# Attention with a bias table in DRAM: shifted rows at one constant distance

## The chip, the cores and the metric

The kernel runs on one core of a Trainium2 chip. The metric is device time of one execution in microseconds; the median of the runs is compared. Inputs and outputs lie in DRAM, and the five engines of the core (TensorE or PE, VectorE or DVE, ScalarE or ACT, GpSimd or POOL, SyncE or SP) run their own instruction streams and meet at semaphores.

## The reference

Attention with a position bias that a small network computes, and behind it a feed-forward part with a cosine gate:

```python
# q, k, v: (4, 8, 576, 64) = batch, heads, positions, head size
scores = scale * np.matmul(q, k.transpose(0, 1, 3, 2))
psi_rel = np.log1p(np.abs(pos[:, None] - pos[None, :]))
psi_i = np.log1p(np.maximum(pos[:, None], 1.0))
x = (psi_rel / psi_i)[..., None]
bias = np.maximum(x @ w1 + b1, 0.0) @ w2        # 32 hidden, 8 heads
scores = scores + bias.transpose(2, 0, 1)[None]
attn = softmax(scores)
x = concat_heads(attn @ v)                      # (2304, 512)
h = x @ w_in                                    # 2048 wide
out = (h * np.cos(h)) @ w_out
```

The bias of a head is a 576 x 576 matrix. It depends on the query position i through `psi_i` and on the distance i - j, and it is the same for all four batches.

## The kernel before, in words

**The bias table.** For one query position the bias of all keys is a window of a row that holds the bias by distance. The kernel computes, for 16 query positions at a time (one of 36 groups), a tile `rt` of 128 rows x 591 numbers: row 8 i + head serves position i of the group and one head. `bias_hid` makes the hidden layer `ht` (three or four instructions on DVE, mostly a fourth on ACT), `bias_rows` multiplies it with the output weights on PE into `pa`, `bias_store` scales it on ACT into `rt` (a pool of 5 buffers) and SP stores it to a DRAM scratch `sc`. Eight groups make one tile t of 128 query positions, `sc[t]`; t = 4 has four groups. The order of the tiles in this stage is 4, 0, 1, 2, 3.

**The load.** `load_bias(hp, t)` fetches the bias of a pair of heads for 128 query positions into `bt` tiles (11 buffers), one for each head: partition i gets the 576 numbers that begin at column 15 - (i mod 16) of its row. The first head is one load of 128 x 576; the second is two loads (64 and 512 columns). For t = 4 both heads share one `bt`, 64 partitions each, one load for each head. The loads for the first pair of heads are issued during the table's stage: t = 4 after row group 11, t = 0 after 19, t = 1 after 27, t = 2 and 3 at its end. The loads for the next pair are issued in the last batch of the pair before it, and used one batch later.

**Attention.** 16 units (4 head pairs x 4 batches), each of 5 slots with the tiles 0, 1, 4, 2, 3. In a slot `qk` multiplies on PE (L390), one DVE instruction for each head adds the bias `bt` and keeps the extreme of each row (L403), ACT does the exponential (L423), POOL divides by the sum (L445), PE turns the result over (L452, L465) and multiplies it with v (L514). The order on every engine is written out in `slot`; PE runs a unit's `qk` ahead of the transposes of the slots before. The first unit has no earlier slots to fill PE with.

**Feed-forward.** The rest, from about 317 us on: two chains of matmuls (L640, L695) on PE, with the gate on ACT and DVE.

**DMA.** All transfers are issued by SP, in program order, with eight semaphores in turn: a transfer waits on SP until the one that was issued eight before it has landed.

Of the kernel before, what the change touches and what calls it, by code (L numbers as in the profile page):

```python
# [9 lines left out]
F32 = mybir.dt.float32  # L10
# [18 lines left out]
def kernel(  # L29
# [11 lines left out]
    nc = tc.nc  # L41
    B, H, S, D = q.shape
# [2 lines left out]
    C = 32  # L45
    HP = H // 2
    NQ = S // 16
    RB = S + 16
    HALF = S // 2
    NF = DFF // 128  # L50
    KD = DM // 128
# [9 lines left out]
    dram = ctx.enter_context(tc.tile_pool(name="dram", bufs=1, space=DRAM))  # L61
# [3 lines left out]
    xT = const.tile([128, HP, NT], F32, name="xT")  # L65
    xs = const.tile([128, 2, KD, TB], F32R, name="xs")
    wpre = [const.tile([128, 2, 2, 512], F32R, name=f"wpre{i}") for i in range(WPRE)]
    sc = [dram.tile([8 if t < 4 else 4, 128, RB], F32, name=f"sc{t}") for t in range(5)]
    groups = [list(range(8 * t, min(8 * t + 8, NQ))) for t in range(5)]

    units = [(hp, b) for hp in range(HP) for b in range(B)]
# [39 lines left out]
    with tc.manual_schedule():  # L111
# [98 lines left out]
        def load_bias(hp, t):  # L210
            if t < 4:
                for h in range(2):
                    bt = bp.tile([128, 576], F32, tag="b", name="bt")
                    src = sc[t]
                    for to, at, n in ((0, 0, S),) if h == 0 else ((0, 512, 64), (64, 0, 512)):
                        nc.sync.dma_start(
                            out=bt[:, to : to + n],
                            in_=bass.AP(
                                src.tensor,
                                src.offset + (2 * hp + h) * RB + 15 + at,  # L220
                                [[128 * RB, 8], [8 * RB - 1, 16], [1, n]],
                            ),
                        )
                    bias[hp, t, h] = bt
            else:
                bt = bp.tile([128, 576], F32, tag="b", name="bt")
                src = sc[t]
                for h in range(2):
                    nc.sync.dma_start(
                        out=bt[64 * h : 64 * h + 64],  # L230
                        in_=bass.AP(
                            src.tensor,
                            src.offset + (2 * hp + h) * RB + 15,
                            [[128 * RB, 4], [8 * RB - 1, 16], [1, S]],
                        ),
                    )
                bias[hp, t, 0] = bt
# [59 lines left out]
        def bias_rows(k, hts):  # L297
            nr = 16 * groups[todo[k][0]][todo[k][1]] + 15
            ps = ps_a.tile([128, 1024], F32, tag="a", name="pa")
            cuts = sorted({0, nr, 512, RB - 1})  # L300
            for a, b in zip(cuts, cuts[1:]):
                for s, ht in enumerate(hts):
                    if a < nr:
                        i = ht[:, nr - b + 1 : nr - a + 1][:, ::-1]
                    else:
                        i = ht[:, a - nr : b - nr]
                    nc.tensor.matmul(  # L307
                        ps[32 * s : 32 * s + 32, a:b],
                        nbd,
                        i,  # L310
                        start=True,
                        stop=True,
                        tile_position=(0, 32 * s),
                    )
            return ps

        def bias_store(k, ps):
            t, gi = todo[k]
            qi = groups[t][gi]
            rt = ra.tile([128, RB], F32, tag="r", name="rt")  # L320
            c = int(k not in ACT_H)
            nc.scalar.activation(  # L322
                out=rt[:, 0 : RB - 1],
                in_=ps[:, 0 : RB - 1],
                func=AF.Identity,
                scale=mrow[:, qi : qi + 1],
                bias=cst[:, c : c + 1],
            )
            nc.sync.dma_start(out=sc[t][gi, :, 0 : RB - 1], in_=rt[:, 0 : RB - 1])

        tiles = [0, 1, 4, 2, 3]
        for i in range(WPRE):
# [6 lines left out]
        for n in range(len(todo) + 1):  # L339
            now = hts  # L340
            if n < len(todo):
                hts = bias_hid(n + 1) if n + 1 < len(todo) else None
                ps = bias_rows(n, now)
            if held:
                bias_store(*held)
            for t in {19: (0,), 27: (1,), 36: (2, 3)}.get(n, ()):
                load_bias(0, t)
            if n == 11:
                load_bias(0, 4)
            held = (n, ps)  # L350
            if n == 6:
                for x in "kq":
                    load(1, x)
            if n in T_FIRST:
                keep_turned(T_FIRST[n][1], turn(*T_FIRST[n], bank()))
            if n in S_FIRST:
                for step in S_FIRST[n][1]:
                    split(0, S_FIRST[n][0], step)
            if n == len(todo):
                abs_w(*wparts[0])  # L360
# [182 lines left out]
        def slot(i):  # L543
# [46 lines left out]
            if now:  # L590
                if i == 1:
                    load(0, "v")
                    load(2, "k")
                for du, x in LOAD_PLAN[j]:
                    if u + du < NU:
                        load(u + du, x)
                hp, b = units[u]
                if b == B - 1 and hp + 1 < HP:
                    load_bias(hp + 1, tiles[j])
                if u == NU - 1 and j < KD:  # L600
                    split_x(0, 0, j)
# [236 lines left out]
```

## Time and profile before

| | |
|---|---|
| runs | 739.06, 742.66 and 959.5 us, median 742.66 |
| the profiled execution | 740.42 us, of which the span from first to last instruction is 738.6 |
| PE | busy 711.1 us, 96% of the span |
| DVE, ACT, POOL | 598.4, 442.5 and 404.3 us |
| mean granted TensorE clock | 0.99 |

The busy shares are means over three stages. In the first 60 us the bias table is made, from 60 to some 317 us attention runs, and from there on the feed-forward part. What a transfer costs is to be read from the stretches in which an engine waited for it, since PE is nearly always busy elsewhere.

### The profile page before, as it was taken

The numbers are of one execution on the slowest core, as the hardware profiler recorded it, in microseconds if no ns is written. First come the engines' busy times: TensorE is split into PE (matmuls) and PEld (weight loads), VectorE is DVE, ScalarE is ACT, GpSimd is POOL, SyncE is SP. The second block draws the span as 40 slices with busy tenths as digits, with TensorE's granted clock in tenths as the row PEclk, the third lists the DMA queues.
The fourth block names the chain that finished last, engine by engine and source line by source line (L and its number), as shares of the span: only waits on it lengthen the run. The fifth ranks groups of instructions, "written<-read, shape, count | busy, mean of one in ns | idle before, by whom it ended". The sixth has DMA issues, their size and how long they took to land.

```text
span 738.6 us, 15708 instructions
## 1 busy us (share of the span) xinstructions
PE 711.1 (96%) x5786; PEld 572.2 (77%) x5786; DVE 598.4 (81%) x1307; ACT 442.5 (60%) x948; POOL 404.3 (55%) x486
## 2 busy tenths in 40 slices
PE   6986999999999999989999999999999999999997
PEld 3764666666666666659899898888888888998985
DVE  8985688889888888846788789898998998966655
ACT  6886678787778888744555555545444454433342
POOL 0204687888877788873546364473555453663300
PEclk9999799999999999999999999999999999999999
DMA  6777426533642640200101010101101010001113
GB/s 200 253 267 194 118 57 159 136 96 92 163 96 67 178 106 18 75 1 1 58 29 58 30 58 28 58 30 48 38 30 57 29 58 29 1 36 51 44 43 87
DMA packets 83918, 58.65 MB, mean 79 GB/s; under 512 B 61824, under 2 KB 70144, under 8 KB 83840
## 3 DMA queue, kind: packets, MB, share of 16 engines
q1 hardware_dynamic: 83840, 57.63, 28.0%
q8 instruction: 46, 0.75, 0.4%
q14 instruction: 32, 0.26, 0.1%
HBM read 42.00 MB, written 15.61 MB: 78 GB/s over the span
## 4 chain that ended last, share of the span: by engine, by line
PE 80%; DMA 8%; DVE 7%; ACT 2%; issue 2%; POOL 0%; SPq 0%; DVEq 0%; ACTq 0%; POOLq 0%
PE ph L640 26%; PE po L695 25%; PE pv L514 10%; PE s L390 9%; DMA bt<-sc 5%; PE pm L452 4%; PE pa L307 3%; DMA sc<-rt 2%; PE pt L465 2%; PE pt L186 1%; DVE P L403 1%; DVE gl L669 1%; DVE ht L291 1%; ACT rt L322 1%; PE spare L186 1%
## 5 line engine op out<-in xcount | busy, mean ns | idle before, releaser
L445 POOL TENSOR_SCALAR P<-P,rc 128x576 f32<-128x576 f32 x144 | 115.3, 813 | 81.1 <-DVE rc L438 33.2
L403 DVE CUSTOM_DVE_ANT_0 P<-s,bt 128x576 f32<-128x576 f32 x144 | 104.1, 754 | 35.9 <-PE s L390 22.1
L644 ACT ACTIVATE a<-ph,quarter 128x384 int32<-128x384 f32 x96 | 55.8, 581 | 108.2 <-PE ph L640 107.0
L650 DVE SCALAR_TENSOR_TENSOR r<-a,ph 128x384 f32<-128x384 int32 x96 | 52.8, 550 | 79.5 <-ACT a L644 79.4
L423 ACT ACTIVATE P<-P,m 128x576 f32<-128x576 f32 x144 | 110.6, 771 | 4.3 <-DVE m L403 3.9
L499 POOL TENSOR_TENSOR xs<-xT,xs 128x384 fp32r<-128x384 f32 x96 | 107.7, 1122 | 8.0
L640 PE MATMUL ph<-xs,wpre 128*128 128x384 f32 x576 | 109.5, 338 | 0.8 <-DVE a L659 0.8
L640 PE MATMUL ph<-xs,w 128*128 128x384 f32 x576 | 108.3, 337 | 0.5 <-DVE a L659 0.5
L640 PEld LDWEIGHTS ph<-xs,wpre 128*128 128x128 f32 x576 | 101.8, 188 | 7.0 <-DVE a L659 2.1
L640 PEld LDWEIGHTS ph<-xs,w 128*128 128x128 f32 x576 | 101.3, 188 | 5.5 <-DVE a L659 1.6
L390 PEld LDWEIGHTS s<-kN,qT 64*128 64x128 f32 (+1 forms) x864 | 71.1, 188 | 43.6 <-DVE m L403 11.0
L655 ACT ACTIVATE r<-r,hpi 128x384 f32<-128x384 f32 x96 | 59.3, 618 | 69.5 <-DVE r L651 69.5
L390 PE MATMUL s<-kN,qT 64*128 64x288 f32 (+1 forms) x864 | 94.3, 316 | 6.4 <-DVE m L403 5.6
L498 POOL TENSOR_SCALAR xs<-xT 128x384 fp32r<-128x384 f32 x96 | 61.8, 644 | 45.3 <-PE ph L640 45.3
L514 PE MATMUL pv<-PT,vN 128*64 128x320 f32 (+1 forms) x512 | 78.5, 429 | 2.3 <-ACT xT L472 2.3
L695 PE MATMUL po<-w,gh 128*128 128x512 f32 x288 | 75.3, 396 | 0.0
L695 PE MATMUL po<-wpre,gh 128*128 128x512 f32 x288 | 75.2, 396 | 0.0
L669 DVE TENSOR_TENSOR gl<-a,gh 128x384 fp32r<-128x384 f32 x96 | 74.4, 775 | 0.6 <-ACT gh L663 0.6
L109 POOL TENSOR_TENSOR w<-wb,w 128x512 fp32r<-128x512 f32 x16 | 20.7, 1296 | 89.9 <-ACT w L107 89.9
L651 DVE SCALAR_TENSOR_TENSOR r<-a,r 128x384 f32<-128x384 int32 x96 | 61.6, 641 | 3.3
L663 ACT ACTIVATE gh<-a 128x384 fp32r<-128x384 f32 x96 | 49.9, 520 | 22.9 <-DVE a L659 22.2
L472 ACT ACTIVATE PT<-pm 128x512 f32<-128x512 f32 (+1 forms) x80 | 44.2, 552 | 30.5 <-PE pm L452 30.1
(83 smaller groups left out, 1205.7 us busy)
## 6 DMA issues: line engine op xcount, KB each, us to landing
sc<-rt SPq DMA_DIRECT2D x36, 295.5 KB
raw<-in_moe_w_in_dram SPq DMA_DIRECT2D x16, 512.0 KB
raw<-in_moe_w_out_dram SPq DMA_DIRECT2D x16, 512.0 KB
bt<-sc SPq DMA_DIRECT2D x16, 288.0 KB
nk<-in_k_dram SPq DMA_DIRECT2D x32, 128.0 KB
nq<-in_q_dram SPq DMA_DIRECT2D x32, 128.0 KB
bt<-sc SPq DMA_DIRECT2D x16, 256.0 KB
vN<-in_v_dram SPq DMA_DIRECT2D x32, 128.0 KB
```

The lines of the kernel that those rows point to most:

```text
L390: nc.tensor.matmul(s[h][:, hf, 0:HALF], qTs[u % 2][r, a, 128 * t : 128 * t + 128] if t < 4 else qTs[u % 2][:, a, 512:640], kN[u][r, b, o : ...
L403: nc.vector.tensor_tensor_reduce(neg.rearrange("p (a x) -> p a x", a=2), s[h][:, :, 0:HALF], bias[hp, t, h].rearrange("p (a x) -> p a x", ...
L423: nc.scalar.activation(out=P[u, j][:, 576 * h : 576 * h + 576], in_=neg, func=AF.Exp, bias=m[:, 0:1], scale=-1.0, accum_out=dn[u, j][:, h ...
L445: nc.gpsimd.tensor_scalar(p, p, r, 1.0, ALU.mult, ALU.mult)
L498: nc.gpsimd.tensor_scalar(h, src, 1.0, 1.0, ALU.mult, ALU.mult)
L499: nc.gpsimd.tensor_tensor(l, src, f(h), ALU.subtract)
L514: nc.tensor.matmul(ps[64 * h : 64 * h + 64, 0 : WQ[hf]], a, m, start=(c == 0), stop=(c == 4), tile_position=(r.start, 64 * h), skip_group_ ...
L640: nc.tensor.matmul(ps, a, x, start=(i == 0), stop=(i == 3 * KD - 1))
L651: nc.vector.scalar_tensor_tensor(r, n, -TWO_PI_LO, r, ALU.mult, ALU.add)
L655: nc.scalar.activation(out=r, in_=r, func=AF.Sin, scale=SIN_SCALE, bias=hpi)
L669: nc.vector.tensor_tensor(gl, a, f(G[key][0]), ALU.subtract)
L695: nc.tensor.matmul(O[n][i], a[:, 128 * i : 128 * i + 128], w, start=(i0 == 0 and p == 0), stop=(i0 == GF - 1 and p == 2),)
```

## The change

The scratch `sc[t]` becomes one row of numbers. A row of the table still has 591 numbers; rows of a group lie 608 numbers apart (`PITCH`), and a group begins 16 x (8 x 608 - 1) numbers behind the one before it (`GP`) where it was 128 x 592. So the start of position i + 1 lies 8 x 608 - 1 numbers behind that of position i for all 128 positions of a tile, over the seams of groups too. The source of a load is then one dimension of 128 rows with n numbers each, where it was 8 groups of 16 rows; for t = 4 it is 64 rows where it was 4 groups of 16. The tile `rt` has 591 columns instead of 592. The numbers that are stored and loaded are the same. Every engine has the same instructions in the same order with the same waits; in the list of SP's transfers the 56 bias loads read 128x576 instead of 128x1x576 (and so on), and nothing else differs.

```diff
-    RB = S + 16
+    RB = S + 15
+    PITCH = S + 32
+    GP = 16 * (8 * PITCH - 1)
...
-    sc = [dram.tile([8 if t < 4 else 4, 128, RB], F32, name=f"sc{t}") for t in range(5)]
+    sc = [dram.tile([1, (8 if t < 4 else 4) * GP + 16], F32, name=f"sc{t}") for t in range(5)]
...
                             in_=bass.AP(
                                 src.tensor,
-                                src.offset + (2 * hp + h) * RB + 15 + at,
-                                [[128 * RB, 8], [8 * RB - 1, 16], [1, n]],
+                                src.offset + (2 * hp + h) * PITCH + 15 + at,
+                                [[8 * PITCH - 1, 128], [1, n]],
                             ),
...
-                            src.offset + (2 * hp + h) * RB + 15,
-                            [[128 * RB, 4], [8 * RB - 1, 16], [1, S]],
+                            src.offset + (2 * hp + h) * PITCH + 15,
+                            [[8 * PITCH - 1, 64], [1, S]],
...
-            cuts = sorted({0, nr, 512, RB - 1})
+            cuts = sorted({0, nr, 512, RB})
...
-                out=rt[:, 0 : RB - 1],
-                in_=ps[:, 0 : RB - 1],
+                out=rt,
+                in_=ps[:, 0:RB],
...
-            nc.sync.dma_start(out=sc[t][gi, :, 0 : RB - 1], in_=rt[:, 0 : RB - 1])
+            nc.sync.dma_start(
+                out=bass.AP(sc[t].tensor, sc[t].offset + gi * GP, [[PITCH, 128], [1, RB]]),
+                in_=rt,
+            )
```

## Rows read from the trace of the kernel before

**Rows 1.** The page, part 4: the chain that ended last, by line.

```profile
PE ph L640 26%; PE po L695 25%; PE pv L514 10%; PE s L390 9%; DMA bt<-sc 5%; PE pm L452 4%; PE pa L307 3%; DMA sc<-rt 2%; PE pt L465 2%; PE pt L186 1%; DVE P L403 1%; DVE gl L669 1%; DVE ht L291 1%; ACT rt L322 1%; PE spare L186 1%
```

**Rows 2.** DMA view, 167.5 to 215.2 us: packets of SP's queue; transfers issued, KB each.

```profile
q1 hardware_dynamic: 12760, 5.84, 51.8%
...
bt<-sc SPq DMA_DIRECT2D x4, 288.0 KB
bt<-sc SPq DMA_DIRECT2D x4, 256.0 KB
vN<-in_v_dram SPq DMA_DIRECT2D x6, 128.0 KB
nq<-in_q_dram SPq DMA_DIRECT2D x6, 128.0 KB
nk<-in_k_dram SPq DMA_DIRECT2D x6, 128.0 KB
raw<-in_moe_w_out_dram SPq DMA_DIRECT2D x1, 512.0 KB
bt<-sc SPq DMA_DIRECT2D x2, 144.0 KB
bt<-sc SPq DMA_DIRECT2D x4, 32.0 KB
vN<-in_v_dram SPq DMA_DIRECT2D x6, 16.0 KB
nk<-in_k_dram SPq DMA_DIRECT2D x3, 32.0 KB
nk<-in_q_dram SPq DMA_DIRECT2D x3, 32.0 KB
```

**Rows 3.** The chain in order of time, 0 to 100 us: start, us, what.

```profile
1.19 3.69 DMA lt<-in_ltab_dram
...
38.98 6.05 DMA sc<-rt
...
60.65 2.90 DMA sc<-rt
...
64.93 8.32 DMA bt<-sc
```

**Rows 4.** Timeline of ACT, 22 to 64 us: start, busy, instruction [idle before, releaser].

```profile
45.14 1.58 ACT L322 ACTIVATE rt<-pa,cst,mrow 128x591 f32<-128x591 f32 x2 [2.54 <-DMA sc<-rt]
...
56.53 2.32 ACT L322 ACTIVATE rt<-pa,cst,mrow 128x591 f32<-128x591 f32 x3 [2.05 <-DMA sc<-rt]
```

**Rows 5.** Timeline of DVE, 22 to 84 us.

```profile
47.27 8.21 DVE L291 TENSOR_SCALAR ht<-lt,edge 128x416 f32<-128x416 f32 x21 [2.28 <-PE pa L307]
60.15 0.76 DVE L403 CUSTOM_DVE_ANT_0 P<-s,bt 128x576 f32<-128x576 f32 x1 [4.67 <-PE s L390]
...
73.42 0.76 DVE L403 CUSTOM_DVE_ANT_0 P<-s,bt 128x576 f32<-128x576 f32 x1 [1.72 <-DMA bt<-sc]
```

**Rows 6.** Windows, four units between their first L403: us, busy (x instructions), clock, DMA.

```profile
75.96:95.08 19.12, 18.08 (x191) 12.51 (x187) 13.42 (x40) 11.94 (x31) 12.42 (x17) 0.84 0.46 110
126.50:142.72 16.22, 15.96 (x184) 10.87 (x182) 13.86 (x40) 13.13 (x35) 12.69 (x17) 1.00 0.64 148
189.96:206.39 16.43, 16.19 (x184) 11.01 (x182) 14.05 (x41) 13.08 (x35) 12.68 (x17) 1.00 0.66 147
253.61:269.31 15.70, 15.70 (x187) 10.84 (x183) 14.08 (x41) 12.62 (x34) 12.91 (x18) 1.00 0.63 156
```

**Rows 7.** Windows around the fall of the clock; columns PE, PEld, DVE, ACT, POOL.

```profile
61.60:71.84 10.24, 7.21 (x80) 5.69 (x81) 7.68 (x22) 8.02 (x23) 7.14 (x10) 1.00 0.74 165
71.84:82.08 10.24, 7.37 (x46) 5.43 (x48) 4.92 (x15) 4.23 (x11) 5.08 (x7) 0.50 0.58 124
```

**Rows 8.** Windows in the table's stage; the last column is GB/s.

```profile
24.00:28.00 4.00, 4.00 (x69) 2.60 (x72) 3.56 (x10) 3.43 (x9) 1.22 (x2) 1.00 0.97 361
41.12:61.60 20.48, 15.74 (x291) 9.67 (x280) 13.36 (x37) 14.95 (x24) 0.00 (x0) 1.00 0.78 272
```

## The prediction

> **What bounds the kernel now.** I read the chain of waits first. It is PE for most of the way, and two DMA lines are the largest things in it that are not PE: the bias loads with 5% and the stores of the table with 2% [rows 1], together some 50 us. That is not what they cost. The chain is followed back through a transfer from its landing to its issue, while PE was mostly at work beside it. So I went on to the views that tell what an engine lost: timelines with the idle time ahead of an instruction, and windows from one attention unit to the next. In the feed-forward part, from about 317 us, no bias load is left; whatever the change does must come from the first 317 us.
>
> Then the question of how a bias load runs. A window of the DMA view that begins and ends in a quiet stretch lets one count [rows 2]. It has 45 transfers. Their rows of data are: bias 12 x 128 and 2 x 64 rows; q, k and v 18 x 512 rows of 256 B; six 16 KB and six 32 KB pieces with 64 and 128 rows; w_out 128 rows. Sum 1536 + 128 + 9216 + 384 + 768 + 128 = 12160. The queue moved 12760 packets, so 600 are not data: one for each DMA engine that ends its share of a transfer. If all 45 ran on 16 engines there would be 720. With 31 others at 16, twelve bias loads at 8 and the two of t = 4 at 4 it is 496 + 96 + 8 = 600, exactly. So a bias load runs on 8 or 4 of 16 engines, the sizes of its outer dimension, and the other transfers, whose outer dimension has 128 or 64 rows, on all.
>
> What that does is seen in the chain: the load of `lt`, also 128 rows of 2304 B, needs 3.69 us, the last bias load before attention 8.32; a store right behind the three loads of t = 0 lands after 6.05 us, one with no load near it after 2.90 [rows 3]. The same engines carry the loads and a half of each store, and what is queued behind waits for them.
>
> **The change, part by part.** The outer dimension becomes 128 (64 for t = 4), so the same data is spread over 16 engines, and a tile's loads occupy an engine half as long, for t = 4 a quarter. Four places gain.
>
> A, the table's stage. ACT fills five `rt` buffers and stands still when the oldest store hasn't landed: 2.54 us before 45.14 and 2.05 before 56.53 [rows 4], behind the loads of t = 0 and t = 1. The first one reaches DVE, the engine that sets the pace there, as 2.28 us of idle time before 47.27. The second falls behind DVE's last `ht` (47.27 + 8.21 = 55.48), where only ACT's stores are left between it and the first `qk`; DVE's first L403 waits for it [rows 5]. The two add: 2.28 + 2.05 = 4.3 us earlier at 60.15. Would a balanced queue still be too slow? DVE makes 21 `ht` in 8.21 us, 3.25 for a row group, so at its undisturbed pace a store of 295.5 KB goes out every 1.27 us, which is 238 GB/s, and a tile's 576 KB of loads in eight groups are 58 more: 296 GB/s. The stage now moves 272, and 361 have been seen over 4 us [rows 8]. So it should fit with little to spare; if 326 were the limit, 5.57 MB of the 20.48 us would need 17.1 and the gain were 3.4. Bounds 2.3 (one wait stays) to 4.6, taken 4.3.
>
> B, the end of the first unit. DVE waits 1.72 us for the load of t = 3 [rows 5]. That load is issued when the last store has landed, and its third piece takes 8.32 us; with 3.69, as for `lt`, it lands 4.6 us earlier [rows 3], more than the wait. The whole stage in front shifts both alike. Taken 1.7, bounds 1 to 2.1.
>
> C, the first unit of each further pair of heads. It takes 16.22, 16.43 and 15.70 us [rows 6]; the third shows the length without a wait. Gain 0.52 + 0.73 = 1.25, bounds 0.8 to 1.3.
>
> D, the clock. [...] With A and B, the same work of the first unit fills 1.7 us less, and the thin time between the last table rows and the second unit shrinks by about 4. I take it that the clock stays up, but this term is all or nothing: 0 or 3.4. [...]
>
> Cost nothing: SP issues the 56 loads at the same places. A shorter issue would only free SP, for which nothing in this argument waits. The loads of q, k and v that are queued behind bias loads lose the less loaded engines and find the others less full; no wait for them stands in this argument. The row distance of 2432 instead of 2368 B leaves the 2364 B that a row writes as they are.
>
> Sum: 4.3 + 1.7 + 1.25 + 3.4 = 10.65 us. Against the profiled execution of 740.42 us that gives 729.8. That execution lies between the two lower runs shown, 739.06 and 742.66, the second of which is the median, so the same 1 or 2 us are uncertain behind the change.
>
> **Rivals.**
> 1. The clock falls all the same: 740.42 - 7.25 = 733.2. For it: the first unit has little for PE to do, and the fall came in its middle. Against it: shorter waits.
> 2. The rate is the limit, not the balance: 16 engines at once pull no more than the 326 to 361 GB/s that were seen, ACT's waits shrink by half, and the clock falls: 740.42 - 2.3 - 1.7 - 1.25 = 735.2.
> 3. The loads don't spread; the split isn't set by the outer dimension. Then nothing changes, 740.4. The count of 600 speaks against it.
> 4. Slower: the stores suffer from the new row distance. The pace of the stage asks 238 GB/s of them; below that the 36 of them set it. At 200 GB/s one takes 1.51 us instead of 1.27, 36 x 0.24 = 8.6 us more, A is gone, and with B and C it is 740.42 + 8.6 - 2.95 = 746.1. For it speaks only that the addresses are new.
>
> [...]
>
> **How the numbers follow.** Forecast (all four terms) 0.50; rival 1 0.27; rival 2 0.13; rival 3 0.06; rival 4 0.04. The predicted time is that of the forecast, 729.8 us. Its own range with the bounds of A to C and the 1 or 2 us between executions is 726 to 733. The range for 8 in 10 goes on through rival 1 and to the edge of rival 2: 726 to 736. Two per cent of 742.66 are 14.9 us, about what a measurement of this kernel can tell from no change; faster by more needs a time below 727.8, which only the lower end of the forecast reaches: 0.16. Slower by over 2% is beyond 757.5, rival 4 at a still lower rate: 0.02. Within: 0.82.
>
> **What would show it.** The packets of SP's queue in the whole program rise by 48 x 8 + 8 x 12 = 480, if all bias loads use 16 engines. ACT's waits for `sc<-rt` (A) and DVE's for `bt<-sc` (B, C) are gone or below a quarter of a microsecond each; the first L403 of DVE stands at about 56 us; the second unit takes some 15.7 us and no window before 317 us has a clock of 0.50 (D). The prediction is wrong if the first L403 comes early and PE's clock falls at another place, or if the stores land later than 3 us with no load near them.

## The result and the profile after

The changed kernel takes 732.16 us (median of 4 runs, 730.09 to 732.7), the kernel before 740.86. The ratio is 0.988, 95% interval 0.985 to 0.992: faster, by some 8.7 us, which is less than 2%. Leaving out executions far off the others (959.5 us here, two of 747 us beside the experiments), before has a median of 739.08 us in the 43 executions beside the experiments (733.82 to 744.69), and the changed program 731.58 in 26 (728.51 to 733.08; 4 of after, 22 of the first four experiments, which came out as the same program): 7.5 us, the better figure for the gain. The profiled execution of after took 731.91 us, 8.51 less than that of before, and its span is 730.1.

**The loads use all 16 DMA engines.** The DMA view of after, over the whole program: packets, MB and share of SP's queue, then transfers with KB each and the median us from issue to landing.

```profile
q1 hardware_dynamic: 84320, 57.63, 27.5%
...
sc<-rt SPq DMA_DIRECT2D x36, 295.5 KB, 3.6
...
bt<-sc SPq DMA_DIRECT2D x16, 288.0 KB, 3.8
...
lt<-in_ltab_dram SPq DMA_DIRECT2D x1, 288.0 KB, 3.9
```

The bytes are the same, the packets 480 more than the 83840 of before, as forecast from the count of [rows 2]. The packets that are not data can be told by their size: in the trace 4960 packets have 4 bytes, 16 for each of SP's 310 transfers; in that of before 4480, which is 254 x 16 + 48 x 8 + 8 x 4, one for each engine as the prediction reads them. A 288 KB bias load lands after 3.8 us, as late as the load of `lt` that has its size.

**Four places, and a fifth.** The timeline of ACT in the table's stage, its two remaining waits for stores (start, busy, instruction, idle before and releaser), which answer to [rows 4]:

```profile
45.53 0.84 ACT L324 ACTIVATE rt<-pa,cst,mrow 128x591 f32<-128x591 f32 x1 [0.48 <-DMA sc<-rt]
...
53.77 3.26 ACT L324 ACTIVATE rt<-pa,cst,mrow 128x591 f32<-128x591 f32 x4 [0.90 <-DMA sc<-rt]
```

And of DVE, answering to [rows 5]:

```profile
48.06 5.82 DVE L293 TENSOR_SCALAR ht<-lt,edge 128x448 f32<-128x448 f32 x15 [0.47 <-PE pa L309]
57.51 0.76 DVE L408 CUSTOM_DVE_ANT_0 P<-s,bt 128x576 f32<-128x576 f32 x1 [3.64 <-PE s L395]
```

The first L408 (L403 before) comes 2.64 us earlier. ACT's waits for stores have shrunk from 6.2 us to 1.4 (view of the tile `sc`), and are not gone. DVE waits for no bias load any more: the view of the tile `bt` names PE and POOL as what DVE waited for, and no DMA.

The windows from unit to unit that answer to [rows 6] (us, busy time of PE, PEld, DVE, ACT, POOL, clock, DMA share, GB/s):

```profile
71.60:89.44 17.84, 17.84 (x189) 12.29 (x185) 13.41 (x40) 11.93 (x31) 12.22 (x16) 0.86 0.40 97
120.86:136.52 15.66, 15.66 (x187) 10.85 (x183) 14.10 (x41) 12.59 (x34) 12.85 (x18) 1.00 0.40 98
183.70:199.68 15.98, 15.95 (x187) 11.02 (x183) 14.33 (x40) 12.60 (x34) 12.88 (x18) 1.00 0.41 96
246.87:262.53 15.66, 15.66 (x187) 10.84 (x183) 14.10 (x41) 12.58 (x34) 12.86 (x18) 1.00 0.40 98
```

The later first units of a pair have lost their waits: 16.22 to 15.66 and 16.43 to 15.98. The second unit, 19.12 before, takes 17.84 with a mean clock of 0.86: the clock fell here too. The windows around it, for [rows 7]:

```profile
59.40:69.64 10.24, 7.60 (x84) 5.77 (x80) 8.38 (x27) 8.66 (x24) 7.57 (x11) 1.00 0.77 200
69.64:76.47 6.83, 6.34 (x42) 4.74 (x44) 3.12 (x9) 2.59 (x7) 4.60 (x6) 0.50 0.52 117
```

It stayed low for 6.83 us where it had been 10.24. The fifth place is the seam from attention to the feed-forward part. The timelines of PE there, of before:

```profile
327.21 3.97 PE L514 MATMUL pv<-PT,vN 128*64 128x320 f32 x16 [2.33 <-ACT xT L472]
```

and of after:

```profile
320.35 2.37 PE L519 MATMUL pv<-PT,vN 128*64 128x320 f32 x16 [2.32 <-ACT xT L477]
```

The same 16 matmuls behind the same wait take 1.6 us less: in the one execution the granted clock was 0.50 from 327.83 to 331.25 us, in the other 1.00 (mean from 313 to 325 us).

The balance of the two spans, 8.54 us: 2.64 up to the first L408, 1.72 in the first unit (15.81 to 14.09), 1.28 in the second, 1.01 in the first units of two pairs, 1.60 at the seam, and 0.29 spread over the rest. Bias loads have gone from 5% of the chain to none among the lines that the page names. Stores of the table are still on it, with 1%; the two large pieces, of the chain in order of time:

```profile
49.43 4.24 DMA sc<-rt
...
54.64 3.19 DMA sc<-rt
```

### The profile page after: what moved, and what is told of

Read it like the earlier page. It is cut to its first block, busy times and chain, and to the rows that moved or that the text cites. A ratio compares the mean times of both kernels' runs of the same rounds, so it can differ in the third digit from the quotient of the medians.

```text
span 730.1 us, 15708 instructions
## 1 busy us (share of the span) xinstructions
PE 708.8 (97%) x5786; PEld 571.9 (78%) x5786; DVE 597.7 (82%) x1307; ACT 441.9 (61%) x948; POOL 403.5 (55%) x486
## 2 busy tenths in 40 slices
DMA packets 84398, 58.65 MB, mean 80 GB/s; under 512 B 62304, under 2 KB 70624, under 8 KB 84320
## 3 DMA queue, kind: packets, MB, share of 16 engines
q1 hardware_dynamic: 84320, 57.63, 27.5%
## 4 chain that ended last, share of the span: by engine, by line
PE 89%; DVE 5%; DMA 2%; issue 1%; ACT 1%; POOL 1%; SPq 0%; DVEq 0%; ACTq 0%
PE ph L645 26%; PE po L700 25%; PE pv L519 12%; PE s L395 11%; PE pm L457 5%; PE pa L309 4%; PE pt L470 2%; PE pt L188 2%; DMA sc<-rt 1%; DVE gl L674 1%; PE spare L188 1%; DVE ht L293 1%; DVE wb L103 1%; DVE acc L723 1%; DMA lt<-in_ltab_dram 1%
## 5 line engine op out<-in xcount | busy, mean ns | idle before, releaser
L450 POOL TENSOR_SCALAR P<-P,rc 128x576 f32<-128x576 f32 x144 | 114.6, 808 | 74.1 <-ACT P L428 29.3
L408 DVE CUSTOM_DVE_ANT_0 P<-s,bt 128x576 f32<-128x576 f32 x144 | 103.8, 754 | 31.1 <-PE s L395 22.5
L519 PE MATMUL pv<-PT,vN 128*64 128x320 f32 (+1 forms) x512 | 76.9, 422 | 2.3 <-ACT xT L477 2.3
```

Of the source, the lines that this page charges most:

```text
L408: nc.vector.tensor_tensor_reduce(neg.rearrange("p (a x) -> p a x", a=2), s[h][:, :, 0:HALF], bias[hp, t, h].rearrange("p (a x) -> p a x", ...
L450: nc.gpsimd.tensor_scalar(p, p, r, 1.0, ALU.mult, ALU.mult)
L519: nc.tensor.matmul(ps[64 * h : 64 * h + 64, 0 : WQ[hf]], a, m, start=(c == 0), stop=(c == 4), tile_position=(r.start, 64 * h), skip_group_ ...
```

## The experiments

The theory: the size of the outer dimension sets how many DMA engines carry a load, and the gain is what the queue of the loaded engines cost. Rival 1: the new row distance does it. Rival 2: a third dimension makes a load slow, whatever its size. The terms of the sum (A, B, C, D) were tested apart. The edits are shown shortened to the places that matter.

**Four kernels that came out as one.** The first four put the groups back into the load, at the constant distance:

```diff
-    [[8 * PITCH - 1, 128], [1, n]],
+    [[16 * (8 * PITCH - 1), 8], [8 * PITCH - 1, 16], [1, n]],    # e1_outer8; 4 of 16 for t = 4
+    [[4 * (8 * PITCH - 1), 32], [8 * PITCH - 1, 4], [1, n]],     # e2_outer32; 16 of 4
+    [[32 * (8 * PITCH - 1), 4], [8 * PITCH - 1, 32], [1, n]],    # e3_outer4; 2 of 32
```

and the fourth, e4_later_pairs, the first of these for the first pair of heads alone.

> The new row distance and the new stores, but the source of a load is again 8 groups of 16 rows (4 of 16 for t = 4), now at the constant distance. Theory (the outer size sets how many DMA engines carry a load): time as before, 740 us (738 to 743), 480 packets fewer than with one dimension, ACT's waits for stores back to about 6 us and DVE's for bias to about 4, first L403 at about 60. Rival 1 (the row distance of 608 numbers did it): time as after, 732. Rival 2 (the number of dimensions makes a load slow): as before, 740, like the theory; the kernel with 32 groups tells these two apart.

> As after, but the source of a load is 32 groups of 4 rows (16 of 4 for t = 4), so it has three dimensions again, with an outer size that 16 divides. Theory: 16 engines, time as after, 732 us (730 to 734), packets 84320. Rival 2 (the third dimension itself costs): 740, waits as before. Rival 1 (row distance): 732 too.

> As after, but 4 groups of 32 rows (2 of 32 for t = 4). Theory: 4 engines (2 for t = 4) carry a load, each twice as long as before. A tile's three loads then hold these engines for about 8 us where they had 4, the stores' rows on the same engines come on top, and a pair of heads needs some 40 us of loads where a unit lasts 15.7: the table's stage 10 to 20 us longer, each of the three changes of pair 15 to 25 us longer, in all 790 to 850 us, and 480 - 208 = 688 packets fewer than after in all (48 x 12 + 8 x 14). Rival 2: 740. Rival 1: 732.

> As after, but the loads for the first pair of heads, which run in the table's stage, have the old 8 groups of 16 (4 of 16). Theory: only the third term of the sum is left, 1 us: time 739.5 (737 to 742), first L403 at about 60 us, DVE waits for bias at the end of the first unit, the later first units of a pair at 15.7 to 16.0 us without a wait. A rival that puts the gain into the later pairs (transfers of q, k and v that land earlier all through attention): 734 or less.

(The 688 packets of the third are 48 x 12 + 8 x 14; the 480 - 208 in its text is a slip.) Measured: 731.65, 732.01, 731.58 and 730.19 us, ratios to before 0.990, 0.991, 0.990 and 0.989, and 84320 packets in each. In these kernels the two dimensions, whose distances fit together, were merged when the kernel was built: SP's transfers read 128x576 in all four, as in after. So the four tell none of the theories apart. They are four more measurements of the changed program, and as such they show how far its executions differ:

| | first L408, us | first two units, us | their mean clock | waits of ACT for stores, us |
|---|---|---|---|---|
| after | 57.51 | 31.93 | 0.89 | 1.4 |
| e1_outer8 | 57.46 | 30.47 | 0.94 | 1.7 |
| e2_outer32 | 58.22 | 30.64 | 0.94 | 3.4 |
| e3_outer4 | 58.65 | 29.33 | 1.00 | 2.4 |
| e4_later_pairs | 57.53 | 29.34 | 1.00 | not named as such |

(In the last, ACT stands idle at the same place, 1.27 us before 53.79, put down to PE.) Before has 60.15, 34.93, 0.85 and 6.2. In the same program the clock fell in the first two units in three of these five executions and stayed up in two.

**Groups that can't be merged.** e5_gap8 leaves 16 numbers unused behind every group:

```diff
-    GP = 16 * (8 * PITCH - 1)
+    GP = 16 * (8 * PITCH - 1) + 16
...
-    [[8 * PITCH - 1, 128], [1, n]],
+    [[GP, 8], [8 * PITCH - 1, 16], [1, n]],      # 4 of 16 for t = 4
```

> The new row distance, the new stores and the tile of 591 columns, but 16 unused numbers behind every group, so that the 8 groups of 16 rows (4 of 16 for t = 4) can't be taken as one dimension; SP's transfers read 128x1x576 again. Theory (the outer size sets how many DMA engines carry a load): time as before, 739 us (736 to 742), 83840 packets, ACT's waits for stores about 6 us, DVE's for bias about 4, first L403 at about 60. Rival 1 (the row distance of 608 numbers did it): 732.

738.02 us, ratio 0.998, interval 0.996 to 1.001: no difference from before. 83840 packets. The view of the tile `sc` (who waited for its transfers, us and times):

```profile
  ACT rt L324: 7.1, 4
  DVE P L408: 1.3, 2
```

Row distance, stores and the tile of 591 columns are those of after, and the gain is gone: rival 1 falls. The slower rival of the prediction falls with the traces: a packet of a stored row (2364 bytes) takes 95 ns in the median in before and in after. DVE's waits are 1.3 us and not the forecast 4; the first L408 came only at 63.27 in this execution, 3 us later than in before, so that the last loads had more time to land; both waits are in later pairs of heads.

e6_gap4 has the unused numbers behind every second group:

```diff
-    sc[t].offset + gi * GP
+    sc[t].offset + gi * GP + gi // 2 * 16
...
-    [[8 * PITCH - 1, 128], [1, n]],
+    [[2 * GP + 16, 4], [8 * PITCH - 1, 32], [1, n]],      # 2 of 32 for t = 4
```

> 16 unused numbers behind every second group: 4 groups of 32 rows (2 of 32 for t = 4). Theory: 4 engines (2 for t = 4) carry a load, 84320 - 688 = 83632 packets. A tile's three loads then hold these engines for some 8 us where they had 4, and a pair of heads needs some 40 us of loads where a unit lasts 15.7: the table's stage and the first unit 15 to 30 us longer, each of the three changes of pair 15 to 25 us longer, in all 790 to 850 us. Rival 2 (a third dimension costs, whatever its size): 739, as with 8 groups.

795.34 us, ratio 1.078, interval 1.075 to 1.081, and 83632 packets, to the packet. The same view for `bt`:

```profile
  DVE P L408: 46.1, 15
```

and the first unit of the second pair of heads, with the one after it:

```profile
137.87:167.00 29.13, 20.27 (x183) 13.92 (x181) 12.77 (x41) 13.82 (x36) 13.32 (x18) 0.79 0.43 118
167.00:184.82 17.82, 17.82 (x191) 12.28 (x187) 13.42 (x41) 11.94 (x31) 12.38 (x17) 0.87 0.32 80
```

A unit that takes 15.66 us with one dimension takes 29.13, with DMA at 0.43 of 16 engines, while DVE waits; a part of it is the clock, 0.79 in the mean. e5 and e6 have the same three dimensions, rows and bytes; only the outer size differs, 8 or 4. So rival 2 falls as the whole cause. A kernel with a third dimension and 16 engines is missing, since e2 was merged, but the packets of the traces show no cost of the dimension itself: a row of 2304 bytes takes 93 ns in after, 96 in e5 and 95 in e6 (medians, 105 to 300 us). With the loads on 16, 8 and 4 engines the time is 732, 738 and 795: from 16 to 8 most is hidden, from 8 to 4 the loads of a pair no longer fit beside one unit.

**A apart from B.** e7_gap_t23 has the unused numbers in tiles 2 and 3 alone:

```diff
+    sc[t].offset + gi * (GP + 16 * (t in (2, 3)))
+    ([[GP + 16, 8], [8 * PITCH - 1, 16]] if t in (2, 3) else [[8 * PITCH - 1, 128]]) + [[1, n]],
```

> Unused numbers behind the groups of tiles 2 and 3 alone; tiles 4, 0 and 1 are loaded in one dimension. Theory by terms: A is kept (the loads of t = 0 and 1 run beside the stores; first L403 at about 57.7, ACT's waits under 2.5 us), B is lost (DVE waits 1 to 2 us for the load of t = 3 in the first unit), C is halved. Time 732 + 1.7 + 0.5 = 734 (732.5 to 737, more where the clock falls for longer). If A were not a matter of the loads of t = 0 and 1 but of the whole layout, ACT's waits would not differ from after.

733.93 us, ratio 0.993, interval 0.989 to 0.997, and 84128 packets, 8 fewer for each of the 24 loads; first L408 at 57.47, ACT's waits 1.5. A is a matter of the loads that run beside the stores, as said. The time came out, B and C did not: there is one wait for bias, of 0.8 us, the first unit takes 14.11 us where after has 14.09, and the first units of the next two pairs 15.68 and 15.97, as in after. The second unit's clock was low here as in after (mean 0.89 over the first two units, 32.02 us). Of the 1.9 us by which this trace is longer than that of after, 1.7 lie behind the last unit's first L408, where the clock was low for 3.41 us at the seam (mean 0.87 from 313 to 326 us).

**What A lacks.** e8_rt9:

```diff
-    ra = opened(stage, "ra", 5, "left")
+    ra = opened(stage, "ra", 9, "left")
```

> After, with 9 buffers for the rows that are stored instead of 5. What is left of ACT's waits for stores (1.4 us in the run of after) goes to zero. Theory (this is what A lacks of its forecast): first L403 at 56.0 to 56.6 instead of 57.5, time 731 (1 us less than after), no more. Rival: the residue only moves on to DVE or PE, first L403 stays at 57 or later and the time at 732.

728.65 us, ratio 0.987, interval 0.985 to 0.990. DVE's timeline:

```profile
27.52 25.60 DVE L293 TENSOR_SCALAR ht<-lt,edge 128x400 f32<-128x400 f32 x67 [0.29 <-PE pa L309]
55.61 0.76 DVE L408 CUSTOM_DVE_ANT_0 P<-s,bt 128x576 f32<-128x576 f32 x1 [2.49 <-PE s L395]
```

DVE makes the last 67 `ht` without a pause, and the first L408 stands at 55.61, where the forecast's A had put it (60.15 - 4.3 = 55.85). The rest of A was the five buffers. The time fell by more than expected, 3.5 us against the median of after. Between the two profiled executions 1.9 us stand before the first L408 and 2.1 in the first two units (29.81 against 31.93), where the low stretch of the clock, 6.83 us in both, here lay in the first unit.

e9_before_rt9 makes the same edit in before.

> Before (8 groups of 16 rows), with 9 buffers for the rows that are stored instead of 5. ACT's waits for stores go to near zero and the first L403 comes at 56 to 57.5, as early as after the change. But the load of t = 3 still lands when eight engines have worked off all that is queued on them. Theory (the loaded engines are the limit, the buffers only pass it on): DVE's waits for bias grow from 4.1 to 6 us or more, the first unit is longer than 16 us, time 738 (736 to 740). Rival (A was only a matter of too few buffers, and the change relieved ACT alone): 735 or less, DVE's waits for bias still at 4.

737.42 us, ratio 0.998, interval 0.995 to 1.001: not told apart from before. First L403 at 55.00, ACT's waits gone, and the first two units longer:

```profile
55.00:91.35 36.35, 29.68 (x288) 21.71 (x287) 23.74 (x73) 22.50 (x58) 21.71 (x29) 0.81 0.54 143
```

36.35 us where before had 34.93 and the one-dimension program 29.3 to 31.9. So 5.15 us are won at the first L403, more than the 4.54 of e8 with the faster loads, and 1.42 given back by the end of the second unit. The time came out as the theory had it; the way only in part: DVE's waits for bias are put at 3.7 us, not at 6 or more, though those of the first unit grew from 2.1 us to 3.1. The comparison with e8, which has the same 9 buffers and the loads on 16 engines, is the clean one: the first unit takes 16.72 us here and 13.63 there, 3.1 less without the waits, at a mean clock of 0.79 and 0.75. The profiled execution is also the fastest of the ten, 733.98 us. How the rest of the 5 us is lost in most of the others stays open; the mean clock of the ten executions is 0.981 to 0.989, against 0.985 to 0.994 in before.

**D, the clock.** e10_fill adds work that nothing reads, where PE waited in the first unit:

```diff
+    FILL = {0: 2, 1: 2, 2: 2, 4: 5}
+    pf = ps_v.tile([128, 512], F32, tag="v", name="fill")
     for i in range(len(jobs)):
         slot(i)
+        for _ in range(FILL.get(i, 0)):
+            nc.tensor.matmul(pf, identr, qTs[0][:, 0, 0:512], start=True, stop=True)
```

> After, with 11 matmuls of 512 columns added on PE in the first unit, into a bank that nothing reads, placed where PE waited (two each behind slots 0, 1 and 2, five behind slot 4). Theory (the fall of the clock comes from the first unit's thin work, not from waits for bias): the clock stays up between 55 and 300 us, the first two units take 29.3 to 29.6 us together, time 731 (730 to 732), some 1 us less than after, whose executions lose 0 to 2.6 us there. Rival: the clock falls as in after, time 732 or, for the added work, above.

730.84 us, ratio 0.988, interval 0.985 to 0.991. The first two units, of e10_fill:

```profile
59.30:88.64 29.34, 27.71 (x299) 19.77 (x298) 23.62 (x73) 21.96 (x58) 21.68 (x29) 1.00 0.60 152
```

With 11 matmuls more the two units take what they take when the clock stays up by itself. In the three profiled executions with this filler (e10 to e12) the clock was 1.00 here; of seven without it (the five of the table, e7 and e8) it fell in five. Three in three could still be chance. The mean clock of every execution is on record and speaks for the filler: it is 0.996 or more in all ten executions of e10 and e11, and in 11 of the 30 of after, e1 to e4 and e8. In the total the gain is 1 us or less, and not told apart from after.

e11_fill_rt9 joins the filler and the 9 buffers.

> One dimension, 9 buffers for the stored rows and the added matmuls of the first unit. If the parts add: first L403 at 55.6, first two units 29.3 us, time 728 (726.5 to 729). If the buffers alone had all there is: 728.7, the same.

728.28 us, ratio 0.985, interval 0.982 to 0.988. First L408 at 55.09, first two units 29.34 us at clock 1.00. It and e8 are the fastest kernels of the study, not told apart from each other.

e12_fill_both adds 28 matmuls of 128 columns at the seam.

```diff
+            if i == 2:
+                pf = ps_m.tile([128, 512], F32, tag="m0", name="fill")
+                for _ in range(28):
+                    nc.tensor.matmul(pf[:, 0:128], identr, identr, start=True, stop=True)
```

> As the one before, and 28 matmuls of 128 columns added where PE waits some 2.3 us at the seam from attention to the feed-forward part (about 315 us). Theory: the low stretch of the clock that most executions have there (3.4 us, 1.6 us of time) is gone: 726.8 (725.5 to 728), no low clock before the last microseconds. Rival: the seam is too long for it to matter, 728.

734.26 us, ratio 0.992: 6 us worse. PE's timeline at the seam of e12_fill_both:

```profile
315.43 6.23 PE L796 MATMUL fill<-identr 128*128 128x128 f32 x28 [1.99 <-ACT PT L477]
321.59 4.12 PE L519 MATMUL pv<-PT,vN 128*64 128x320 f32 x16
```

The filler itself waited 1.99 us for ACT, whose copy `PT` had to read out the bank that the filler writes, so PE stood idle as before; then it took 6.23 us, in a stretch with a mean clock of 0.72 (308 to 326 us), ahead of the matmuls it should have helped. One of the six executions kept a mean clock of 1.00; it took 729.75 us, no less than e11. The theory of the seam is not settled by this.

## Why the prediction was right, and where its terms were off

The direction, the size (732.16 in 726 to 736, forecast 729.8) and the mechanism held. Of the sum of 10.65 us the two profiled executions show 8.5, of which 1.6 are not the change's, and the medians of many executions 7.5. Of the signs that were named, the packets came and DVE's waits for bias went; ACT's waits (0.48 and 0.90 us, not below a quarter), the first L408 (57.51, not 56) and the second unit (17.84 us with a stretch at 0.50, not 15.7) did not come as said.

- **The count of engines** held to the packet: +480 in after, 83840 in e5, 83632 in e6, 84128 in e7. These are the counts for 16 engines with an outer size of 128 or 64 (after), 8 with 8 and 4 with 4 (e5), and 4 with 4 and 2 with 2 (e6). Other outer sizes did not run, and which engines carried a load no row shows.
- **A, forecast 4.3 with bounds of 2.3 to 4.6, measured 2.64** (1.5 to 2.7 over the five executions, in e2 and e3 below the bounds). This is the step that was mis-sized: "so it should fit with little to spare" took two waits as gone, and the view of ACT's waits has 1.4 to 3.4 us of the 6.2 left in the executions that name them. The forecast weighed the rate in GB/s; five buffers are a matter of how long one store is under way. ACT and SP in after, around the second wait that is left:

```profile
46.80 0.83 ACT L324 ACTIVATE rt<-pa,cst,mrow 128x591 f32<-128x591 f32 x1
...
46.76 2.57 SPq L218 DMA_DIRECT2D bt<-sc  x3
49.43 7.95 SPq L331 DMA_DIRECT2D sc<-rt  x9
```

  ACT has written the tile at 47.63. Its store is issued at 49.43, behind the three loads of t = 1, and lands 4.24 us later, at 53.67; ACT, which needs this buffer next, goes on at 53.77. So "SP, for which nothing in this argument waits" was wrong too: the store waited 1.8 us for SP's turn. In before the same store waited 1.5, so what it gained did not come from cheaper issue. The mechanism was the right one: e5 brings the waits back, e7 keeps A with the first loads alone, and e8 shows the full term once the five buffers don't limit. But e9 shows that nine buffers alone bring the first L403 as early: A is a wait that either remedy takes away.
- **B, forecast 1.7, measured 1.72.** The mechanism is shown by e9 against e8 (3.1 us of waits, a first unit 3.1 us longer). That the size agrees is luck: in e5 no such wait came at the end of the first unit, in e7 0.8 us of waiting made it no longer, and in both profiled executions a part of the first unit ran at a clock of 0.50 (from 71.84 us in before, 69.64 in after; with the clock up throughout it takes 13.55 us in e3 and 13.56 in e4). The next thing late at the end of the first unit is POOL, not a transfer: PE's scores for the second unit wait for POOL's split of q, as the timeline of PE in after has it.

```profile
70.13 1.33 PE L395 MATMUL s<-kN,qT 64*128 64x288 f32 x8 [1.20 <-POOL qT L178]
```

- **C, forecast 1.25, measured 1.01.** The second of the two units has 15.98 us without any wait for bias; its undisturbed length is not that of the third, which the term had assumed. Nor is the gain there in every execution: with loads on eight engines these two units took 16.22 and 16.43 us in before, 15.69 and 16.63 in e5, 15.65 and 16.03 in e9. C is worth 0 to 1 us.
- **D, forecast 3.4 as all or nothing, measured 1.28** in the profiled execution, and by the table anything up to the whole: the first two units took 31.93, 30.47, 30.64, 29.33 and 29.34 us. The 3.4 is 19.12 - 15.70, the second unit of before against the last of [rows 6]; where the clock stayed up, the second unit took 15.78 us (29.33 - 13.55 in e3, 29.34 - 13.56 in e4), 3.34 less than in before. "I take it that the clock stays up" was the wrong step; between the forecast and the first rival there is a middle that neither named. Rival 1 counted the shorter waits against the fall, but DVE's wait of 1.72 us [rows 5] lasted from 71.70 to 73.42, so it began 0.14 us ahead of the fall at 71.84 and lay almost wholly behind it. A wait for bias is not needed for the fall: in after there is none in the first unit, and it fell at 69.64 us, after a stretch in which PE was busy for 7.60 of 10.24 us; the idle time of PE next to the fall, 1.20 us up to 70.13, was a wait for POOL. With more work for PE in the first unit the clock stayed up, as the filler shows (1.00 over the first two units of e10 to e12, a mean of 0.996 or more in all ten executions of e10 and e11), so its thin work is a cause. That the loads count as well is seen in the mean clock of whole executions: with loads on eight engines it was never above 0.994 (0.985 to 0.994 in the 43 of before, 0.987 to 0.994 in the ten of e5, 0.992 to 0.994 in the six of e7, which has them in two tiles), and with one dimension it was above that in 16 of 26 (0.989 to 0.997). Which of their effects on the first units does it is open.
- **Not forecast: 1.60 at the seam.** It isn't the change's. The clock fell at the seam in before, e1 to e4, e6 and e7 (3.41 us at 0.50 in each; the windows of 12 us around it in e1, e3 and e4 have a mean clock of 0.86, as in before), and not in after, e5 and e8 to e11; loads on eight engines are in both groups. The two profiled executions therefore differ by 1.6 us more than the change explains.

So the change is worth about 2 us in the table's stage, 3 to 5.6 in the first two units, and up to 1 later, 5 to 8.6 in all against the one profiled execution of before; where in this range is up to the clock, above all. Before varies from one execution to the next as well (733.82 to 744.69 us), and its mean clock explains little of that: the fastest of the 43 has 0.992, one of 742.15 us 0.989.

## What to carry to other kernels

Here a source that was cut into 8 or 4 groups used that many DMA engines by the count of packets, and what was queued behind it waited, stores of another tile too (ACT's waits for stores were 6.2 us in before and 7.1 in e5, 1.4 in after): count packets against rows of data to see it, and try a layout with a long outer dimension, 128 or 64 here. Price a transfer by the stretches in which an engine stood still for it, not by its share of the chain: 7% of the chain, some 50 us, were worth 7.5 to 8.7. And where two waits hang on one queue and a small pool of buffers, a faster queue and more buffers belong together: here, against the 739 us of before beside the experiments, the buffers alone gave 1.7 us, which could not be told from nothing, the loads 7.5 and both 10.4.

## What the runs showed of the hardware

- Issuing a load of 128 rows in one dimension was mostly cheaper for SP than one in 8 groups, 430 ns against 584 in the median. From the views of `bt`, before, then after (min/median/max ns):

```profile
L216 SPq DMA_DIRECT2D bt<-sc x48: 574/584/637, 37.0 to 259.3; - x48
```

```profile
L218 SPq DMA_DIRECT2D bt<-sc x48: 319/430/1542, 37.5 to 249.3; - x48
```

  The three longest of after, 1181 to 1542 ns, stand at 46.8 us, among the table's stores, and at 115.4 and 235.4, where there are none; why is not shown. Groups have long ones too, up to 1193 ns in e5. The loads of 64 rows (t = 4) did not get cheaper: median 562 ns before, 595 after.
- A low clock cost as much as PE had to do in it. In e5 the mean clock of the first two units is 0.81, lower than before's 0.85, and they take 30.34 us, 1 us more than the 29.33 of e3 with the clock up, for the low stretch (13.65 us, from 61.03 on) lies in the thin first unit and just ahead of it. In before, whose low stretch of 10.24 us reaches into the second unit, that unit takes 19.12 us instead of 15.78.
- Halving the engines of a load need not show, halving them again can: in this kernel loads on 8 of 16 engines cost 1% of the time, on 4 they cost 9%.
